# Loading the first input chunk of a split Fourier stage one unit earlier, ahead of the middle stage's loads

## The chip, the cores and the metric

The kernel runs on one core of a Trainium2 chip. Its engines are TensorE (PE in the profile; the weight loads of its matmuls have a row of their own, PEld), VectorE (DVE), ScalarE (ACT), GpSimd (POOL) and SyncE (SP), which here only issues DMAs. The metric is the device time of one execution in microseconds, the median of several runs. All data are float32.

## The reference

Two steps follow each other. The first is a global filter along the sequence: for each of 8 batches and 256 channels, a real Fourier transform over 3008 positions, a product with a complex filter, and the transform back. The second treats the 8 x 3008 = 24064 rows as tokens of a two-layer network with the activation h - tanh(h).

```python
X = np.fft.rfft(x, axis=1)                       # x: (8, 3008, 256)
y = np.fft.irfft(X * (filt_r + 1j * filt_i), n=3008, axis=1)
h = y.reshape(24064, 256) @ w_in                 # w_in: (256, 2048)
out = (h - np.tanh(h)) @ w_out                   # w_out: (2048, 256)
```

## The kernel before

The sequence length is factored as 64 x 47, and the transform is done by matmuls with small Fourier matrices, in stages that meet in DRAM. For batch `b`:

- The first stage turns `x` into the DRAM tensor `ct1[b]`. For batches 3 to 7 it is the generator `split_first` (line 306). It has three chunks `c`. Each chunk loads a piece of the matrix into a tile `f` (line 313) and two tiles `x0` and `x1`, both named `x_sb` in the profile (lines 320, 324, 326: eleven DMAs with the one for `f`, all on SP's queue); then DVE forms `x0 + x1` into a tile `a1` (line 331) and `x0 - x1` in place (line 333); 64 small matmuls follow into four PSUM banks with the tags `t`, `o1`, `y` and `o0` (line 340, tile `pm`); ACT and DVE combine the banks (lines 345 to 349), and eight stores to `ct1[b]` are put at the head of a list of stores. The tiles `f` and `x_sb` have two buffers each, so a new chunk's pair takes the place of the pair before.
- The middle stage, the generator `middle` (line 467), reads `ct1[b]` into a tile `a2` (line 374, four DMAs) and the filter into `ft` (line 382, 1 MB), works in four steps with matmuls at line 401, and writes `ct2[b]`.
- `last` (line 565) reads `ct2` by `load_e2` (lines 553 and 555) and makes the tokens' inputs with the matmuls of line 576.

The two-layer network is most of the work. Its tokens are cut into 48 groups (`groups`: batch `p` by chunk `c` of 0 to 5), and each group into four units `u` of 512 hidden columns. One loop over all 192 units `U` runs three things at once: `up` (first layer, matmuls at line 617, into banks `x`, `y`, `z`) for unit `U`, `shrink` (the activation, ACT lines 729 to 735, DVE line 739, and four GpSimd operations at lines 597 to 600) for unit `U - 1`, and `down` (second layer, matmuls at line 787, into banks `o0` to `o3`) for unit `U - 2`.

The instruction order on every engine is the order in which the program is written; nothing reorders it. Inside `up` there are five points `t(0)` to `t(4)`. Each issues up to four DMAs from the list of stores (line 894) on SP's queue and then takes one step of another generator. Which one is fixed by tables: if `(c, u, k)` is in the set `SPLIT_AT`, the next step of `split_first` for batch `p + 2` is taken, otherwise perhaps a step of `middle` for batch `p + 1`. A step of `split_first` is one of five per chunk: loads, sum, difference, matmuls with half of the combination, the other half. `SPLIT_AT` has 15 places for its 3 x 5 steps, and they hold for `p` = 1 to 5. Its first places are, in the order in which they are met:

```python
(0, 0, 2)  loads of chunk 0        (0, 1, 0)  sum, line 331
(0, 1, 1)  difference, line 333    (0, 1, 3)  matmuls, line 340
```

At the beginning of the last unit of the last group of a batch (`u == 3`, `c == 5`) the generators for the next batch are made. That of `middle` takes its first step there, which issues the loads of `a2` and `ft`; that of `split_first` is only made.

```python
if u == 3 and c + 1 == NC and p + 2 < BATCH:
    mids[p + 2] = middle(p + 2, zd4)
    next(mids[p + 2])
if u == 3 and c + 1 == NC and p + 3 < BATCH:
    firsts[p + 3] = split_first(p + 3, zd4)
```

SP's queue issues its DMAs strictly in order. Each of them waits on one of eight semaphores that are taken in turn, so a DMA is not issued before the one eight places ahead of it has landed.

Of the kernel before, what the change touches and what calls it, by code (L numbers as in the profile page):

```python
# [116 lines left out]
def kernel(  # L117
# [188 lines left out]
    def split_first(b, z):  # L306

        quarters = [slice(32 * k, 32 * k + 32) for k in range(4)]
        for c, tags in enumerate((("t", "o1", "y", "o0"), ("t", "o3", "o1", "o2"),
                                  ("t", "o1", "y", "o0"))):  # L310
            f = tr.tile([128, XH, 128], F32, tag="f", bufs=2, name="f")[:, 0:2]
            f = f.rearrange("p a (b n) -> p (a b) n", n=32)
            nc.sync.dma_start(f, split_d[:, 256 * c:256 * c + 256])
            x0, x1 = (tr.tile([128, XH, DM], F32, tag="x", bufs=2, name="x_sb") for _ in range(2))
            for h, t in enumerate((x0, x1)):
                at = b * SEQ + 32 * h * NR
                for g in range(2):
                    r = 2 * FH * c + FH * g
                    low, high = quarters[g], quarters[2 + g]
                    nc.sync.dma_start(t[low], dram(x.tensor, (at + r) * DM,  # L320
                                                   [[NR * DM, 32], [1, FH * DM]]))
                    lo = int(r == 0)
                    if lo:
                        nc.sync.dma_start(t[high, 0], dram(x.tensor, at * DM,
                                                           [[NR * DM, 32], [1, DM]]))
                    nc.sync.dma_start(t[high, lo:FH], dram(x.tensor, (at + NR - r - lo) * DM,
                                                           [[NR * DM, 32], [-DM, FH - lo], [1, DM]]))
            yield
            both = tr.tile([128, 2, 2, DM], F32, tag="a1", bufs=1, name="a1")
            even = both.rearrange("p v n c -> p (v n) c")  # L330
            V.tensor_add(even, x0, x1)
            yield
            V.tensor_sub(x1, x0, x1)
            yield
            banks = z(tags)
            for n in range(2):
                for k, (bank, part) in enumerate(zip(banks, quarters)):
                    for j, to in enumerate(quarters):
                        m, odd = 2 * (j // 2) + n, j % 2
                        nc.tensor.matmul(bank[to, n], f[part, 2 * m + odd],  # L340
                                         (x1 if odd else even)[part, m], start=True, stop=True)
            made = both, x0.rearrange("p (v n) c -> p v n c", v=2)
            other = x1[:, 0:2]
            for g, a1 in enumerate(made):
                ACT.copy(a1[:, 1], banks[2 + g])
            ACT.copy(other, banks[1])
            for g, a1 in enumerate(made):
                V.tensor_add(a1[:, 0], other if g else banks[0], a1[:, 1])
                V.tensor_sub(a1[:, 1], other if g else banks[0], a1[:, 1])
                outs[:0] = [(dram(ct1[b], ((1 - j % 2) * NH + 2 * FH * c + FH * g +  # L350
                                           2 * (j // 2)) * DM,
                                  [[2 * NH * DM, 32], [64 * NH * DM, 2], [1, 2 * DM]]),
                             a1[part].rearrange("p v n c -> p v (n c)"))
                            for j, part in enumerate(quarters)]
                yield

    SPLIT_AT = {(0, 0, 2), (0, 1, 0), (0, 1, 1), (0, 1, 3), (1, 1, 1), (1, 1, 4), (2, 0, 2),
                (3, 0, 2), (4, 2, 0), (4, 2, 2), (4, 3, 0), (5, 0, 2), (5, 1, 0), (5, 1, 3),
                (5, 2, 2)}

# [187 lines left out]
    def load_e2(b, c, parts=None, tiles=None):  # L548

        e2, gt = tiles or (tr.tile([128, CH, DM], F32, tag="e2", bufs=2, name="e2"),  # L550
                           tr.tile([128, CH, 64], F32, tag="gt", bufs=2, name="gt"))
        if tiles is None:
            nc.sync.dma_start(gt, (pairs_d if b else g_d)[:, CH * 64 * c:CH * 64 * (c + 1)])
        if parts is None:
            nc.sync.dma_start(e2, dram(ct2[b], CH * c * DM,
                                       [[(PAD if b else NH) * DM, 128], [1, CH * DM]]))
        return e2, gt
# [431 lines left out]
    with tc.tile_pool(name="tr", bufs=2) as tr, tc.manual_schedule():  # L989
# [260 lines left out]
        with tc.tile_pool(name="dn", bufs=2) as dn, \  # L1250
# [69 lines left out]
            for U in range(total + 2):  # L1320
                i, u = divmod(U, 4)
                if U == 6:
                    assert not pending
                    late = (None for u in (3, 5, 6, 7) for _ in sums(u))
                if U == 3:
                    G.dma_start(mats[:, 0:10 * PAD], wide_d[0:KM])
                if U < total:
                    p, c = groups[i]
                    if c == 0 and u == 0 and 0 < p < BATCH - 1:
                        plan += STAGES  # L1330
                    if u == 0 and i + 1 < len(groups) and c + 1 < NC:
                        e2s[i + 1] = load_e2(*groups[i + 1])
                    if u == 2 and i + 1 < len(groups) and c + 1 == NC:
                        assert not plan
                        e2s[i + 1] = load_e2(*groups[i + 1])
                    if u == 3 and c + 1 == NC and p + 2 < BATCH:
                        mids[p + 2] = middle(p + 2, zd4)
                        next(mids[p + 2])
                    if u == 3 and c + 1 == NC and p + 3 < BATCH:
                        firsts[p + 3] = split_first(p + 3, zd4)  # L1340
                sh = shrink(U - 1) if 0 <= U - 1 < total else iter(())
                dw = iter(())
                if 0 <= U - 2 < total:
                    dw = (down if U - 2 >= 4 else down_plain)(U - 2)

                def converting(n):

                    for _ in range(n):
                        if next(late, pending) is pending:
                            pending.clear()  # L1350

                def d():

                    next(dw, None)

                def e():

                    next(dw, None)
                    converting((U < 6) * (3 if U > 1 else 1))

                def s():

                    next(sh, None)

                def t(k):

                    store_some(4)
                    if k == 2 and stores:
                        store(*stores.pop())
                    if U >= total:  # L1370
                        return
                    pos = 20 * c + 5 * u + k
                    if i == 1 and pos == LEAD - 7:
                        assert not any(pending)
                        mids[1] = middle(1, zd4)
                        next(mids[1])
                        plan.extend(STAGES)
                    if (u, k) == (3, 2) and i + 1 < len(groups):
                        next(last(i + 1, z2))
                    elif due and due[0] <= pos and (U < 4 or u < 3 and k == 2):  # L1380
                        due.pop(0)
                        next(firsts[2])
                    elif (c, u, k) in SPLIT_AT and 0 < p < BATCH - 2:
                        next(firsts[p + 2])
                    elif plan and plan[0] == kinds.get((u, k)):
                        plan.pop(0)
                        next(mids[p + 1])
                    converting(2)
                    if k and U > 1:
                        next(copies, None)  # L1390
                        next(copies, None)

                if U < total:
                    if U == total - 1:
                        ones = cst.tile([128, 1], F32, name="ones")
                        G.memset(ones, 1.0)
                    (up if U >= 4 else up_plain)(U, d, e, s, t)
                else:
                    for k in range(5):
                        s()  # L1400
                        s()
                        d()
                        if U == total + 1 and k in (0, 2):
                            next(bound)
                        e()
                        t(k)
# [39 lines left out]
```

## Time and profile before

| | |
|---|---|
| median of 3 runs | 2573.39 us (2572.35 to 2575.72) |
| profiled execution | 2572.9 us, of which the span is 2571.1 us |
| TensorE matmul busy | 2542.1 us, 99% of the span |
| VectorE, ScalarE, GpSimd busy | 73%, 65%, 57% |
| granted TensorE clock, mean | 0.998 |
| DMA | 212.43 MB, 83 GB/s over the span |

All times in rows of the profile are microseconds from the start of the span unless they say ns. In a row of the timeline the columns are start, length, engine, line, operation, output and inputs, and the number of instructions merged into the row; in square brackets stands how long the engine was idle before and what ended that. A row of waits has who waited, for whom, the sum, the number of times and the longest one. A row of the windows view has the stretch, its length, the busy time of each engine with its number of instructions, the granted clock, and the DMA share and rate. Ends of matmuls are modelled, and a few records can be missing. One unit takes some 13 us, one batch of 24 units some 310 us.

### The profile page before, as it was taken

The numbers are of one execution on the slowest core, as the hardware profiler recorded it, in microseconds if no ns is written. First come the engines' busy times: TensorE is split into PE (matmuls) and PEld (weight loads), VectorE is DVE, ScalarE is ACT, GpSimd is POOL, SyncE is SP. The second block draws the span as 40 slices with busy tenths as digits, with TensorE's granted clock in tenths as the row PEclk, the third lists the DMA queues.
The fourth block names the chain that finished last, engine by engine and source line by source line (L and its number), as shares of the span: only waits on it lengthen the run. The fifth ranks groups of instructions, "written<-read, shape, count | busy, mean of one in ns | idle before, by whom it ended". The sixth has DMA issues, their size and how long they took to land.

```text
span 2571.1 us, 44601 instructions
## 1 busy us (share of the span) xinstructions
PE 2542.1 (99%) x17076; PEld 2171.9 (84%) x17076; DVE 1873.6 (73%) x2265; ACT 1667.3 (65%) x2497; POOL 1476.6 (57%) x1124
## 2 busy tenths in 40 slices
PE   8999999999999999999999999999999999999998
PEld 7678888888888888888888888888889888898887
DVE  6878777887678876788668886688866877555555
ACT  4566666666666666666666666666666666666665
POOL 4356665666456655566656665466645766555552
PEclk9999999999999999999999999999999999999999
DMA  8973214422343323342333322343123322110110
GB/s 222 270 186 102 64 41 102 119 66 54 77 113 91 81 53 86 89 105 69 72 88 88 99 67 60 94 111 95 37 60 90 93 66 50 28 32 18 26 21 19
DMA packets 333660, 212.43 MB, mean 83 GB/s; under 512 B 231738, under 2 KB 304856, under 8 KB 329790
## 3 DMA queue, kind: packets, MB, share of 16 engines
q1 hardware_dynamic: 318511, 184.59, 29.5%
q0 software_dynamic: 11424, 17.03, 2.5%
q10 hardware_dynamic: 3502, 7.87, 0.9%
q8 instruction: 136, 2.23, 0.4%
q14 instruction: 87, 0.70, 0.1%
HBM read 128.75 MB, written 83.39 MB: 83 GB/s over the span
## 4 chain that ended last, share of the span: by engine, by line
PE 87%; DMA 4%; DVE 3%; SPq 2%; POOL 1%; issue 1%; ACT 0%; DVEq 0%; POOLq 0%; ACTq 0%
PE o L787 40%; PE x L617 23%; PE z L617 11%; PE y L617 6%; PE pm L401 3%; PE pu L576 2%; SPq L894 1%; DMA ft<-filt 1%; PE pm L340 1%; DMA filt<-in_filt_r_dram 1%; DMA filt<-in_filt_i_dram 1%; DVE h L739 1%; DMA x<-in_x_dram 0%; DMA x_sb<-in_x_dram 0%; DMA a<-in_moe_w_out_dram 0%
## 5 line engine op out<-in xcount | busy, mean ns | idle before, releaser
L787 PE MATMUL o<-t,wd 128*128 128x256 f32 (+1 forms) x3008 | 763.2, 376 | 0.0
L597 POOL TENSOR_TENSOR t<-h 128x512 f32<-128x512 f32 (+1 forms) x186 | 305.8, 1644 | 707.1 <-DVE h L739 697.8
L739 DVE TENSOR_TENSOR h<-h,y 128x1024 f32<-128x1024 f32 (+1 forms) x384 | 579.1, 1508 | 159.4 <-ACT y L735 155.9
L787 PEld LDWEIGHTS o<-t,wd 128*128 128x128 f32 x3008 | 568.4, 190 | 86.3 <-POOL o L815 15.1
L617 PE MATMUL x<-tu,wu 128*128 128x256 f32 (+1 forms) x2256 | 576.2, 378 | 0.0
L787 PE MATMUL o<-h,wd 128*128 128x256 f32 (+1 forms) x2256 | 573.3, 377 | 1.8 <-DVE h L739 1.8
L787 PEld LDWEIGHTS o<-h,wd 128*128 128x128 f32 x2256 | 425.2, 190 | 73.6 <-issue 18.4
L623 ACT COPY s<-x 128x512 f32<-128x512 f32 (+1 forms) x188 | 108.8, 579 | 566.0 <-PE x L617 565.5
L617 PEld LDWEIGHTS x<-tu,wu 128*128 128x128 f32 x2256 | 423.0, 190 | 57.6 <-issue 3.9
L732 ACT ACTIVATE y<-y 128x1024 f32<-128x1024 f32 (+1 forms) x384 | 399.4, 1040 | 12.1
L735 ACT ACTIVATE y<-y 128x1024 f32<-128x1024 f32 (+1 forms) x384 | 399.8, 1041 | 4.6
L729 ACT ACTIVATE y<-h 128x1024 f32<-128x1024 f32 (+1 forms) x384 | 400.5, 1043 | 3.5 <-DVE h L665 1.7
L598 POOL TENSOR_TENSOR t<-h,t 128x512 f32<-128x512 f32 (+1 forms) x186 | 310.6, 1670 | 14.6
L600 POOL TENSOR_TENSOR t<-h,t 128x512 f32<-128x512 f32 (+1 forms) x186 | 301.5, 1621 | 0.0
L599 POOL TENSOR_TENSOR t<-h 128x512 f32<-128x512 f32 (+1 forms) x186 | 289.9, 1558 | 0.0
L623 ACT COPY u<-x 128x512 f32<-128x512 f32 (+1 forms) x376 | 213.7, 568 | 56.8 <-PE x L617 54.0
L665 DVE COPY h<-x 128x512 f32<-128x512 f32 (+1 forms) x188 | 127.8, 680 | 127.1 <-PE x L617 127.0
L617 PE MATMUL y<-ut,wu 128*128 128x256 f32 (+1 forms) x752 | 190.1, 375 | 0.8 <-ACT a L299 0.8
L617 PE MATMUL z<-ut,wu 128*128 128x256 f32 (+1 forms) x752 | 190.2, 375 | 0.5 <-DVE h L657 0.4
L617 PE MATMUL x<-ut,wu 128*128 128x256 f32 (+1 forms) x752 | 190.1, 375 | 0.6 <-DVE h L665 0.6
L617 PE MATMUL z<-tu,wu 128*128 128x256 f32 (+1 forms) x752 | 190.1, 375 | 0.4 <-DVE h L673 0.4
L657 DVE TENSOR_TENSOR h<-z,u 128x512 f32<-128x512 f32 (+1 forms) x188 | 127.2, 676 | 77.4 <-ACT u L623 77.1
(198 smaller groups left out, 2812.3 us busy)
## 6 DMA issues: line engine op xcount, KB each, us to landing
ft<-filt SPq DMA_DIRECT2D x28, 1024.0 KB
ct<-nn SPq DMA_DIRECT2D x56, 512.0 KB
e<-ct SPq DMA_DIRECT2D x47, 512.0 KB
a<-ct SPq DMA_DIRECT2D x112, 192.0 KB
out_dram<-ot SPq DMA_DIRECT2D x1248, 16.0 KB
x_sb<-in_x_dram SPq DMA_DIRECT2D x110, 128.0 KB
ct<-a SPq DMA_DIRECT2D x60, 128.0 KB
ct<-x_sb SPq DMA_DIRECT2D x60, 128.0 KB
```

Of the source, the lines that this page charges most:

```text
L597: by.tensor_sub(t[0], b[0][1], b[0][0])
L598: by.tensor_sub(t[1], b[1][1], t[0])
L599: by.tensor_sub(t[2], b[1][1], b[0][1])
L600: by.tensor_sub(t[3], b[1][0], t[1])
L617: nc.tensor.matmul(bank[:, k], wu[:, q - 1, (2 * u + k) * 128:(2 * u + k + 1) * 128], rhs[q - 1], start=(first and k == 0), stop=True, ski ...
L623: ACT.copy(t, X)
L665: V.tensor_copy(h[:, 2, :, 0:w], X)
L729: ACT.activation(y[k], ht[k], AF.Arctan, scale=TURN)
L732: ACT.activation(y[k], y[k], AF.Tanh, scale=BEND)
L735: ACT.activation(y[k], y[k], AF.Square, scale=SCALE, accum_out=y_sums[:, 2 * U + k // 2:2 * U + k // 2 + 1])
L739: V.tensor_mul(ht[k], ht[k], y[k])
L787: nc.tensor.matmul(product(q), wd[:, q - 1, (2 * u + k) * 128: (2 * u + k + 1) * 128], rhs[q - 1][:, k], start=(u == 0 and k == 0 and q == ...
```

## The change

The first step of `split_first` (the eleven loads of chunk 0) is taken where the generator is made, at the beginning of the last unit of the preceding batch's last group, and it is taken before the first step of `middle`, so that on SP's queue its eleven loads stand ahead of the loads of `a2` and `ft`. One place is taken out of `SPLIT_AT`, (0, 1, 1). The steps that remain for chunk 0 move forward by one place: the sum is taken at (0, 0, 2), the difference at (0, 1, 0); the matmuls stay at (0, 1, 3), and the other twelve steps stay where they were.

```diff
-    SPLIT_AT = {(0, 0, 2), (0, 1, 0), (0, 1, 1), (0, 1, 3), (1, 1, 1), (1, 1, 4), (2, 0, 2),
+    SPLIT_AT = {(0, 0, 2), (0, 1, 0), (0, 1, 3), (1, 1, 1), (1, 1, 4), (2, 0, 2),
                 (3, 0, 2), (4, 2, 0), (4, 2, 2), (4, 3, 0), (5, 0, 2), (5, 1, 0), (5, 1, 3),
                 (5, 2, 2)}
...
                         e2s[i + 1] = load_e2(*groups[i + 1])
+                    if u == 3 and c + 1 == NC and p + 3 < BATCH:
+                        firsts[p + 3] = split_first(p + 3, zd4)
+                        next(firsts[p + 3])
                     if u == 3 and c + 1 == NC and p + 2 < BATCH:
                         mids[p + 2] = middle(p + 2, zd4)
                         next(mids[p + 2])
-                    if u == 3 and c + 1 == NC and p + 3 < BATCH:
-                        firsts[p + 3] = split_first(p + 3, zd4)
```

No instruction is added or removed on any engine except for waits. On DVE, the order of the first two units of a batch becomes (line numbers of the kernel before): 739, **331**, 657, 665, 739, 673, **333**, 640, 802, 739, 808; it was 739, 657, 665, 739, 673, **331**, 640, 802, **333**, 739, 808.

## The prediction

> **What bounds the kernel now.** I read the page first: who is busy, and the chain that ended last.
>
> ```profile
> span 2571.1 us, 44601 instructions
> PE 2542.1 (99%) x17076; PEld 2171.9 (84%) x17076; DVE 1873.6 (73%) x2265; ACT 1667.3 (65%) x2497; POOL 1476.6 (57%) x1124
> PE 87%; DMA 4%; DVE 3%; SPq 2%; POOL 1%; issue 1%; ACT 0%; DVEq 0%; POOLq 0%; ACTq 0%
> ```
>
> TensorE is the bound nearly everywhere, so this change can win only the moments in which TensorE stands, or lose by making new ones. The view of waits says where the split first stage (lines 331 to 340) makes such moments.
>
> ```profile
> DVE a L331 <- DMA x_sb<-in_x_dram: 24.6, 4, 6.7
> PE pm L340 <- DVE o L808: 2.6, 4, 0.7
> PE pm L340 <- DVE x_sb L333: 0.8, 2, 0.5
> ```
>
> VectorE waits four times for `x` to land, 24.6 us in all, and behind this TensorE waits at the stage's matmuls. Four times, but the stage runs in five batches (`p` = 1 to 5): one batch shows it without the wait. To price the difference I took the stretch of each batch's first group, from the first matmul of one line 576 block to the first of the next, in the windows view. The rows are `p` = 1 to 5.
>
> ```profile
> 400.39:449.42 49.03, 49.03 (x386) 44.35 (x385) 36.61 (x45) 32.63 (x53) 25.89 (x21) 1.00 0.35 89
> 708.27:759.49 51.22, 50.17 (x385) 44.48 (x384) 33.91 (x46) 32.61 (x53) 24.04 (x21) 1.00 0.41 100
> 1018.35:1069.70 51.35, 50.17 (x385) 44.47 (x384) 33.91 (x46) 32.62 (x53) 24.01 (x21) 1.00 0.41 98
> 1328.56:1378.89 50.33, 49.62 (x386) 44.40 (x385) 33.93 (x46) 32.62 (x53) 24.02 (x21) 1.00 0.41 99
> 1637.74:1687.82 50.08, 49.57 (x385) 44.35 (x384) 33.93 (x46) 32.62 (x53) 24.01 (x21) 1.00 0.42 100
> ```
>
> The same work takes 49.03 us where VectorE does not wait and 51.22, 51.35, 50.33 and 50.08 where it does, at a granted clock of 1.00 in all of them. The whole excess lies at the line 340 block: from the last matmul group ahead of it to the first behind it is 2.28 us in `p` = 1 (427.07 to 429.35) and 4.50 in `p` = 2 (734.95 to 739.45).
>
> ```profile
> 427.07 0.92 PE L617 MATMUL x<-tu,wu 128*128 128x224 f32 x4
> ...
> 429.35 1.13 PE L787 MATMUL o<-t,wd 128*128 128x256 f32 x4
> ```
>
> ```profile
> 734.95 0.92 PE L617 MATMUL x<-tu,wu 128*128 128x224 f32 x4
> ...
> 739.45 1.13 PE L787 MATMUL o<-t,wd 128*128 128x256 f32 x4
> ```
>
> **The change part by part.** *The loads, 20 us earlier.* The timelines of SP and of VectorE in `p` = 2 show why `x` is late, with two rows of the chain for what lands when.
>
> ```profile
> 701.44 1.90 SPq L894 DMA_DIRECT2D out_dram<-ot  x4
> 703.82 1.73 SPq L374 DMA_DIRECT2D a<-ct  x4
> 705.60 0.38 SPq L382 DMA_DIRECT2D ft<-filt  x1
> ...
> 725.13 0.43 SPq L313 DMA_DIRECT2D f<-f_split  x1
> ...
> 730.88 0.42 SPq L326 DMA_DIRECT2D x_sb<-in_x_dram  x1
> ```
>
> ```profile
> 705.60 8.69 DMA ft<-filt
> ...
> 730.88 2.38 DMA x_sb<-in_x_dram
> ```
>
> ```profile
> 722.65 0.62 DVE L657 TENSOR_TENSOR h<-z,u 128x448 f32<-128x448 f32 x1 [1.25 <-ACT u L623]
> ...
> 726.24 0.62 DVE L673 TENSOR_TENSOR h<-z,u 128x448 f32<-128x448 f32 x1
> 733.48 1.23 DVE L331 TENSOR_TENSOR a<-x_sb 128x1024 f32<-128x1024 f32 x1 [6.62 <-DMA x_sb<-in_x_dram]
> ...
> 737.62 0.42 DVE L808 TENSOR_TENSOR o<-o,p 128x256 f32<-128x256 f32 x1
> ```
>
> The eleven loads are issued from 725.13, the last at 730.88, and it lands 2.38 us later, at 733.26; VectorE stood ready at 726.86 (726.24 + 0.62). It stands 6.62 us, and queued behind line 331 are 640, 802, 333, 739 and 808. Line 808 empties PSUM bank `o1`, which line 340 overwrites, so TensorE goes on only after 737.62 + 0.42 = 738.04. After the change the loads stand where 374 begins now, 703.82 (the copies into `ct1` that line 374 waits for are also the last readers of the tile, so nothing waits longer). Issuing them takes 730.88 + 0.42 - 725.13 = 6.2 us, to 710.0, and with the 2.38 the last lands at about 712.4. VectorE reaches line 331 at its new place when it falls idle before line 657, at 722.65 - 1.25 = 721.40: 9 us to spare. In `p` = 3 to 5 the program is the same, and the loads land with the same margin: the whole 24.6 us of waiting go.
>
> *What is late next: the PSUM banks.* `p` = 1 answers it: line 331 without a wait, line 808 done before the block.
>
> ```profile
> 419.03 1.91 DVE L331 TENSOR_TENSOR a<-x_sb 128x1024 f32<-128x1024 f32 x1
> ...
> 426.40 0.41 DVE L808 TENSOR_TENSOR o<-o,p 128x256 f32<-128x256 f32 x1
> ```
>
> Line 808 ends at 426.40 + 0.41 = 426.81, before TensorE so much as begins the group ahead of the block, at 427.07. So no wait of that kind is left, and 49.03 us is the level: gain (51.22 + 51.35 + 50.33 + 50.08) - 4 x 49.03 = **6.86 us**. `p` = 1 gains nothing, since it has no wait to lose.
>
> Does a later wait take it back? The stretch is bounded by blocks of TensorE, whose work outside it is unchanged, and `p` = 1 and 2 go on from it with no stall carried over: the excess is in the stretch and no shorter one follows. I count the whole.
>
> A second, smaller price comes from TensorE's idle rows alone: 2.6 + 0.8 = 3.4 us. They count the time after the modelled end of a matmul; the stretches go by starts, so I take 6.86 and keep 3.4 as the lower end. The Trainium skill, "Perfetto Trace Analysis", section "Tensor Engine Instruction (MATMUL, LD_WEIGHTS)", says that the start of a matmul is recorded but its end is computed from its size. By that rule idle rows undercount; the trace agrees, 2.2 us more from start to start in `p` = 2 where the busy column leaves 51.22 - 50.17 = 1.05.
>
> *Line 331, ahead of 657.* At 721.40 VectorE is idle until 722.65, and 1.23 us fits there to 0.02. The profile's group view gives the length of line 331 over all chunks, and GpSimd's timeline what runs beside it.
>
> ```profile
> L331 DVE TENSOR_TENSOR a<-x_sb x15: 1211/1226/2301, 419.0 to 1908.9; 128x1024 f32<-128x1024 f32 x15
> ```
>
> ```profile
> 726.47 1.27 POOL L597 TENSOR_TENSOR t<-h 128x512 f32<-128x512 f32 x1 [6.16 <-DVE h L739]
> ```
>
> It can take 2.30 us. Then 657 ends at 721.40 + 2.30 + 0.62 = 724.32, and the matmuls that overwrite its bank `z` follow at 725.23:
>
> ```profile
> 725.23 0.92 PE L617 MATMUL z<-ut,wu 128*128 128x224 f32 x4
> ```
>
> That leaves 0.9 us: cost 0. GpSimd is idle from 720.31 to 726.47, so I expect 1.23.
>
> *Line 333, ahead of 640 and 802.* It now starts at 726.24 + 0.62 = 726.86, beside GpSimd's run from 726.47, so up to about 2.3 us, to 729.2; 640 follows to 729.8. The next writer of its bank `y` is line 340, behind the group of 734.95: cost 0. Lines 802 and 808 no longer have 333 between them, so 808 comes sooner than in `p` = 1, if at all different.
>
> Were both moved operations at their longest and their slacks gone, the excess over 1.21 us would fall on TensorE: 2 x (2.30 - 1.21) x 5 batches = 10.9 us. With slacks of 0.9 us and 5 us none of it does. The Trainium skill, "SBUF — State Buffer", section "Who interferes with whom", speaks against the two moves: a VectorE operation with two SBUF inputs and a GpSimd operation that reads SBUF hold each other off for a whole instruction. The trace agrees that line 331 has two lengths.
>
> *What waits behind the eleven loads on SP.* `a2`, `ft`, 20 output stores, and `gt` and `e2` of the next group are issued 6.2 us later, and a little more, since at most eight DMAs are on the way at once. The `ft` load lands at 714.29 now and would at about 720.5. Their users:
>
> ```profile
> 742.78 1.37 PE L401 MATMUL pm<-a,mats_sb 24*32 24x512 f32 x32
> ```
>
> Line 401 needs `a2` at 742.78 (740.6 after the gain), `ft` later still: 20 us of cover. `e2`, issued ahead of 725.13 now, is read by the line 576 block at 759.49 that ends the stretch of `p` = 2: 34 us ahead now, some 26 then. If that cover were gone each microsecond would be one of TensorE in each of five batches. By the time of the stores that follow, SP has made up the 6.2 us, because the eleven loads are missing there. In `p` = 0 the first loads move into batch 0's last unit; same order, same cover. Cost 0. The few waits added to instructions (line 340 and a transpose now name DMAs which landed long before) I bound by line 331, which starts at 733.48, 0.22 us after its last load landed at 733.26, with all its waits: at two such instructions in five batches 0 to 2.2 us. I take 0: a wait on something long done is nearer to a check than to that row, which ends a real wait.
>
> **Sum.** 2572.9 - 6.86 = 2566.0 for the profiled execution, which stands 0.5 us under the median of 2573.39; against the median, 2566.5 us, or 0.27% faster.
>
> **The rivals.** A difference under 0.2%, 5.1 us, is about what a measurement of this kernel cannot tell from none.
>
> *Half the gain.* TensorE gains only its idle rows, 3.4 us, because another wait takes the place of 808's at the block: 2570.0 us. For it: the block waits for several VectorE results. Against: `p` = 1, the same program, 49.03 us.
>
> *Late at the new place (slower).* The loads might not have landed at 721.40, because they wait for the copies out of the old tile and share the DMA engines with `a2` and `ft`. Then line 657 stands behind 331, and `z` is freed late. It decides when `x` lands after 725.23 - 0.62 - 1.23 = 723.4, that is 11 us later than I reckon. With as long a wait as now, 6.62, 331 would start at 728.0, `z` be free at 729.9, and TensorE lose 4.7 us in each of five batches: 23.5 - 6.9 = 16.6 slower, 2590 us. Against: the whole set lands within 8.1 us of its first issue in `p` = 2.
>
> *The pair exclusion*, as priced above: 2566.5 + 10.9 = 2577. It needs both slacks gone.
>
> *It changes nothing.* If the matmul block was limited by other evictions, all four excesses would remain: 2573. `p` = 1 speaks against it.
>
> **How the numbers follow.** Full gain 0.69, half 0.15, nothing 0.05, late 0.06, exclusion 0.05. The full case has its own range, 2564.5 to 2568.5: the sum with up to 2 us for the added waits downwards of the gain, 1.5 us for the spread of medians, and some tenths more from an earlier 808. With 0.15 and 0.05 of the others taken in, the range is 2564.0 to 2573.0, a little over 0.8 of the cases. Faster by over 0.2% needs 5.1 of the 6.9 us; a few of the full cases fall under it: 0.65. Within 0.2%: 0.24. Slower: 0.11.
>
> **What would show it.** Right: no row of line 331 waiting for `x`; line 340 without the waits for 808 and 333; the four stretches at 49.0 us; the eleven loads on SP's timeline ahead of line 374 and `ft` landing some 6 us later with no reader waiting. Wrong: a wait of 331 at its new place, a wait of TensorE's `z` or `y` matmuls for 657 or 640, or one of line 401 for `a2`; or stretches above 50 us with the waits gone, which would put the excess elsewhere than VectorE's lateness.

## The result, and the profile after

The changed kernel takes 2564.38 us (median of 7 runs, 2563.03 to 2568.16) against 2573.39 us (7 runs, 2571.99 to 2577.16): a ratio of 0.9967, 95% interval 0.9955 to 0.9978. It is faster by 9.0 us, where 6.9 were forecast. From the page of its profiled execution, the span, the busy time of each engine, and the chain that ended last by engine:

```profile
span 2564.4 us, 44624 instructions
...
PE 2540.9 (99%) x17076; PEld 2177.8 (85%) x17076; DVE 1878.4 (73%) x2265; ACT 1666.3 (65%) x2497; POOL 1481.4 (58%) x1124
...
PE 94%; DMA 2%; DVE 1%; ACT 1%; issue 1%; POOL 0%; ACTq 0%; POOLq 0%; DVEq 0%
```

The share of TensorE in the chain that ended last goes from 87% to 94%; the shares of DMA (4% to 2%), of VectorE (3% to 1%) and of SP's queue (2% to none in this line) are the main ones that shrink. The five stretches, in the windows view of the changed kernel:

```profile
400.99:450.01 49.02, 49.02 (x386) 44.38 (x385) 35.30 (x45) 32.61 (x53) 25.72 (x21) 1.00 0.38 86
708.86:757.88 49.02, 49.02 (x385) 44.37 (x384) 35.33 (x46) 32.61 (x53) 25.73 (x21) 1.00 0.43 102
1016.74:1065.76 49.02, 49.02 (x386) 44.38 (x385) 35.33 (x46) 32.60 (x53) 25.73 (x21) 1.00 0.45 103
1324.61:1373.63 49.02, 49.02 (x386) 44.38 (x385) 35.31 (x46) 32.62 (x53) 25.71 (x21) 1.00 0.44 100
1632.48:1681.50 49.02, 49.02 (x385) 44.38 (x384) 35.31 (x46) 32.61 (x53) 25.71 (x21) 1.00 0.45 101
```

All five are 49.02 us, with TensorE busy throughout. Batch 2 of the changed kernel (its first group begins 0.59 us later in the span, at 708.86 instead of 708.27), on SP's queue:

```profile
703.96 0.44 SPq L313 DMA_DIRECT2D f<-f_split  x1
...
708.96 0.42 SPq L326 DMA_DIRECT2D x_sb<-in_x_dram  x1
709.42 1.71 SPq L374 DMA_DIRECT2D a<-ct  x4
711.18 0.38 SPq L382 DMA_DIRECT2D ft<-filt  x1
711.60 14.22 SPq L894 DMA_DIRECT2D out_dram<-ot  x20
```

The timeline of VectorE in the same place, and of TensorE where it overwrites the banks that VectorE frees:

```profile
719.98 1.99 DVE L739 TENSOR_TENSOR h<-h,y 128x1024 f32<-128x1024 f32 x1 [2.31 <-ACT y L735]
721.90 1.21 DVE L331 TENSOR_TENSOR a<-x_sb 128x1024 f32<-128x1024 f32 x1
723.23 0.63 DVE L657 TENSOR_TENSOR h<-z,u 128x448 f32<-128x448 f32 x1
...
727.36 2.04 DVE L333 TENSOR_TENSOR x_sb<-x_sb 128x1024 f32<-128x1024 f32 x1
729.33 0.61 DVE L640 TENSOR_TENSOR h<-y,s 128x448 f32<-128x448 f32 x1
...
733.93 0.42 DVE L808 TENSOR_TENSOR o<-o,p 128x256 f32<-128x256 f32 x1 [1.21 <-ACT p L807]
```

```profile
725.82 0.92 PE L617 MATMUL z<-ut,wu 128*128 128x224 f32 x4
726.57 0.92 PE L617 MATMUL x<-ut,wu 128*128 128x224 f32 x4
...
735.54 0.92 PE L617 MATMUL x<-tu,wu 128*128 128x224 f32 x4
...
737.81 1.13 PE L787 MATMUL o<-t,wd 128*128 128x256 f32 x4
738.78 0.92 PE L617 MATMUL z<-ut,wu 128*128 128x224 f32 x4
...
741.14 1.47 PE L401 MATMUL pm<-a,mats_sb 24*32 24x512 f32 x32
```

Line 331 fills the gap that VectorE had ahead of line 657 and does not wait: by the trace's semaphore updates the last `x` load lands at 713.34, 8.6 us before line 331 starts at 721.90. That is the smallest margin of the five batches; the others have 10.3 to 13.5 us. Line 808 is done at 734.35, before the group of 735.54, and TensorE passes the block in 2.27 us (735.54 to 737.81), without a row that waits for VectorE.

### The profile page after: what moved, and what is told of

Read it like the earlier page. It is cut to its first block, busy times and chain, and to the rows that moved or that the text cites. A ratio compares the mean times of both kernels' runs of the same rounds, so it can differ in the third digit from the quotient of the medians.

```text
span 2564.4 us, 44624 instructions
## 1 busy us (share of the span) xinstructions
PE 2540.9 (99%) x17076; PEld 2177.8 (85%) x17076; DVE 1878.4 (73%) x2265; ACT 1666.3 (65%) x2497; POOL 1481.4 (58%) x1124
## 4 chain that ended last, share of the span: by engine, by line
PE 94%; DMA 2%; DVE 1%; ACT 1%; issue 1%; POOL 0%; ACTq 0%; POOLq 0%; DVEq 0%
PE o L787 43%; PE x L617 25%; PE z L617 12%; PE y L617 6%; PE pm L401 3%; PE pu L576 2%; DMA ct<-a 1%; PE pm L340 1%; DMA raw<-in_moe_w_in_dram 0%; DMA fh<-f 0%; DMA mats_sb<-mats 0%; PE pe L1089 0%; PE o L842 0%; PE pf L297 0%; PE warm L1038 0%
## 5 line engine op out<-in xcount | busy, mean ns | idle before, releaser
L597 POOL TENSOR_TENSOR t<-h 128x512 f32<-128x512 f32 (+1 forms) x186 | 305.7, 1643 | 712.4 <-DVE h L739 703.9
```

Of the source, the lines that this page charges most:

```text
L597: by.tensor_sub(t[0], b[0][1], b[0][0])
```

## The experiments

Two questions: is VectorE's lateness at the block the whole cause, and why is the measured gain 9.0 us when the stretches give 6.9? Stretches of the experiments are from the start of one line 576 block to the next, as in the prediction.

**Behind the middle stage's loads.** The two first steps swapped:

```diff
-  if u == 3 and c + 1 == NC and p + 3 < BATCH:
-      firsts[p + 3] = split_first(p + 3, zd4)
-      next(firsts[p + 3])
   if u == 3 and c + 1 == NC and p + 2 < BATCH:
       mids[p + 2] = middle(p + 2, zd4)
       next(mids[p + 2])
+  if u == 3 and c + 1 == NC and p + 3 < BATCH:
+      firsts[p + 3] = split_first(p + 3, zd4)
+      next(firsts[p + 3])
```

> The changed kernel with the two generators' first steps swapped: the eleven loads of chunk 0 are issued at the same unit, but behind the loads of a2 and ft instead of ahead of them. Theory (only the landing before line 331's place counts): the loads are issued some 2.2 us later and share the engines with ft, land some 4 to 8 us later than in the changed kernel, at about 716 to 720 in batch 2, still ahead of 721.9 where VectorE reaches line 331; all five first-group stretches stay at 49.0 us and the time is that of the changed kernel, 2564 to 2567 us, ratio to the kernel before about 0.9970. Rival (the place ahead of the middle stage's loads is needed): line 331 waits again, line 657 behind it frees bank z late, the stretches go over 49.5 us.

2564.78 us (7 runs), 0.9957 (0.9941 to 0.9972) of the kernel before, whose 21 runs in this series have a median of 2575.41 us. All five stretches are 49.02 us. SP and VectorE in its batch 2:

```profile
704.57 0.38 SPq L382 DMA_DIRECT2D ft<-filt  x1
...
715.46 0.42 SPq L326 DMA_DIRECT2D x_sb<-in_x_dram  x1
```

```profile
720.26 1.21 DVE L331 TENSOR_TENSOR a<-x_sb 128x1024 f32<-128x1024 f32 x1
```

Behind `ft` the last `x` load is issued 8.1 us later than in the changed kernel by the start of the group (715.46 - 707.23 = 8.23 us behind it, against 708.96 - 708.86 = 0.10). It lands at 717.87, 2.4 us before line 331. In batches 1 to 5 this margin is 5.1, 2.4, 1.8, 1.3 and 0.4 us, where the changed kernel has 13.5, 8.6, 10.3, 10.9 and 10.9. So the place ahead of the middle stage's loads is worth no time in these runs, since nothing waits in either order, but it is worth most of the margin: in batch 5 of this variant the loads are just in time.

**The loads alone.** Sum and difference stay where the kernel before has them:

```diff
-    SPLIT_AT = {(0, 0, 2), (0, 1, 0), (0, 1, 3), (1, 1, 1), ...
+    SPLIT_AT = {(0, 1, 0), (0, 1, 1), (0, 1, 3), (1, 1, 1), ...
```

> Only the loads are moved: issued where the changed kernel has them, while the sum and the difference are taken at the places of the kernel before, (0, 1, 0) and (0, 1, 1). Theory (VectorE's wait for x was the whole cause): stretches of 49.0 us in all five batches, as batch 1 of the kernel before had them with these places, ratio about 0.9970, and the time within 1 us or so of the changed kernel. Rival (the earlier sum and difference carry part of the gain, by taking 333 out from between 802 and 808): line 340 waits for 808 or 813 again, stretches of 49.1 to 50 us, 1 to 4 us of the gain missing.

2565.96 us (9 runs), 0.9960 (0.9947 to 0.9973). Five stretches of 49.02 us. In its batch 2:

```profile
727.99 2.04 DVE L331 TENSOR_TENSOR a<-x_sb 128x1024 f32<-128x1024 f32 x1
...
731.44 2.05 DVE L333 TENSOR_TENSOR x_sb<-x_sb 128x1024 f32<-128x1024 f32 x1
...
735.49 0.41 DVE L808 TENSOR_TENSOR o<-o,p 128x256 f32<-128x256 f32 x1
```

Line 808 comes 0.9 us later than in the changed kernel by the start of the group (735.49 - 709.48 = 26.0 against 733.93 - 708.86 = 25.1), and that is still early enough. So the move of sum and difference carries none of the gain that these runs can show: the wait for `x` was the cause.

**Four sums, and two.** The sum of chunk 0 repeated at its place, with no value changed:

```diff
-            V.tensor_add(even, x0, x1)
+            for _ in range(4 if c == 0 else 1):
+                V.tensor_add(even, x0, x1)
```

> The changed kernel with the sum of chunk 0 (line 331) computed four times over at its place, which lengthens it by 3 x 1.21 = 3.6 us and changes no value. It measures the slack that the prediction put behind this place. Theory: line 331 starts at 721.9 in batch 2, four of them end at 726.7, line 657 ends at 727.4, and the z matmuls due at 725.8 start 1.6 us late: stretches of 50.6 us in all five batches, 5 x 1.6 = 8 us on top of the changed kernel, about 2572 us. Rival A (VectorE's idle time covers it all): 49.0 us and 2564 us. Rival B (there is no slack): 3.6 us per batch, 18 us, 2582 us.

> The changed kernel with the sum of chunk 0 computed twice, 1.2 us longer, no value changed. The slack behind the place of line 331 by the trace of the changed kernel: line 657 ends at 723.86 in batch 2 and the z matmuls are due at 725.84, 1.98 us. Theory (the slack is real): stretches of 49.0 us in all five batches. Rival (every VectorE microsecond at this place counts): 50.2 us, 6 us in all.

With four sums the time is 2573.81 us (10 runs), 0.9991 (0.9980 to 1.0002), and the stretches are 50.79, 50.80, 50.78, 50.79 and 50.79 us, 1.77 above 49.02. The extra line shifts the numbers below it by one, so 658 and 618 here are 657 and 617 elsewhere:

```profile
726.02 4.99 DVE L332 TENSOR_TENSOR a<-x_sb 128x1024 f32<-128x1024 f32 x4
730.93 0.62 DVE L658 TENSOR_TENSOR h<-z,u 128x448 f32<-128x448 f32 x1
```

```profile
731.61 1.02 PE L618 MATMUL z<-ut,wu 128*128 128x224 f32 x4 [1.51 <-DVE h L658]
```

With two sums (2566.35 us, one run) the stretches are 49.02, 49.02, 49.02, 49.03 and 49.02. Three more sums add 4.99 - 1.21 = 3.78 us to VectorE and 1.77 to TensorE: the slack is 2.0 us, as the trace has it (line 657 ends at 723.86, `z` is due at 725.82), and what goes beyond it falls on TensorE (3.78 - 1.77 = 2.0), in the bank that the prediction named.

**Late at the new place, on purpose.** Loads at the beginning of the batch itself, sum at its new place:

```diff
-    SPLIT_AT = {(0, 0, 2), (0, 1, 0), (0, 1, 1), (0, 1, 3), ...      # kernel before
+    SPLIT_AT = {(0, 0, 0), (0, 0, 2), (0, 1, 0), (0, 1, 3), ...
```

> The rival of the prediction that the loads land late at the new place of the sum, made on purpose: loads at (0, 0, 0) of the batch itself, sum at (0, 0, 2), difference at (0, 1, 0). The loads are issued only some 2 us earlier than in the kernel before and should land at about 731.4 in batch 2, while VectorE stands at line 331 from 721.9. Theory (line 657 is queued behind 331 and frees bank z): the z matmuls of line 617, due at 725.8, start after 731.4 + 1.2 + 0.6 = 733.3, so 7.5 us more in each of batches 2 to 5 and 1 to 2 us in batch 1: stretches of 56 to 58 us, 2564 + 4 x 7.5 + 1.5 = 2596 us, slower than both kernels. Rival (TensorE has other cover there, only the line 340 block matters): stretches under 51 us and a time under 2573 us.

2610.41 us (4 runs), 1.0135 (1.0111 to 1.0159): slower, by the mechanism expected, and by more. The stretches are 54.53, 58.78, 59.53, 58.87 and 57.89 us, in batches 2 to 5 8.9 to 10.5 above 49.02 where 7.5 were expected, and 5.5 in batch 1 where 1 to 2 were. TensorE in batch 2, and three windows of it:

```profile
736.36 1.86 PE L617 MATMUL z<-ut,wu 128*128 128x224 f32 x4 [6.89 <-DVE h L657]
738.01 1.70 PE L617 MATMUL x<-ut,wu 128*128 128x224 f32 x4
```

```profile
728.00:730.00 2.00, 1.47 (x8) 1.01 (x6) 0.00 (x0) 0.00 (x0) 0.00 (x0) 1.00 0.75 197
...
738.00:740.00 2.00, 2.00 (x7) 1.78 (x6) 1.75 (x2) 0.25 (x1) 1.81 (x2) 0.50 0.04 8
...
742.00:744.00 2.00, 2.00 (x11) 1.87 (x10) 0.27 (x1) 0.79 (x3) 2.00 (x2) 1.00 0.00 0
```

The wait for line 657 is there, 6.89 us of idle time. At its end and behind it the granted clock is 0.50, and the group of `z` takes 1.65 us from its start to the next one's (736.36 to 738.01), where in the changed kernel it takes 0.75 us (725.82 to 726.57). This second part of the cost was in no sum of mine. The two parts add up: from the start of the group the `z` matmuls begin 7.05 us later than in the changed kernel (736.36 - 712.35 = 24.01 against 725.82 - 708.86 = 16.96), close to the 7.5 expected; and the clock is at half from 734.86 to 741.69, 5.3 us of it behind the start of `z`, which at half speed loses 2.7. Together that is 9.7 of the 9.8 us.

**The loads of the middle stage late.** In the changed kernel, the first step of `middle` is taken at (0, 1, 4) of the batch that uses it:

```diff
   if u == 3 and c + 1 == NC and p + 2 < BATCH:
       mids[p + 2] = middle(p + 2, zd4)
-      next(mids[p + 2])
...
+  if (c, u, k) == (0, 1, 4) and 0 < p < BATCH - 1:
+      next(mids[p + 1])
```

> The changed kernel with the first step of the middle stage, the loads of a2 and ft, taken at (0, 1, 4) of the batch that uses them instead of a unit before it: behind the stores of the line 340 block on SP's queue, some 30 us later than in the changed kernel. It shows what the cover of these loads is and what it costs when it is gone. Theory: issued at about 742 in batch 2, a2 lands at about 745, where line 401 is due at 740.6: TensorE waits some 4 to 5 us in each of six batches, 24 to 30 us in all, about 2590 us; ft lands some 9 us after its issue and holds only VectorE. Rival (nothing in the middle stage is due so soon): stretches of 49 us, 2564 us.

2625.0 us (one run). The stretches are 60.62, 61.33, 59.97, 60.99 and 59.75 us, 57.6 us over five times 49.02, where 24 to 30 us were expected over six batches. Batch 6, which has no split stage, keeps its 47.2 us: no stores of that stage stand ahead of the loads, and they are issued 10.3 us after the start of its first group, against 32.9 us in batch 2 (754.64 - 721.70). In batch 2:

```profile
754.64 1.75 SPq L374 DMA_DIRECT2D a<-ct  x4
```

```profile
758.17 6.63 PE L401 MATMUL pm<-a,mats_sb 24*32 24x512 f32 x32 [4.12 <-DMA a<-ct]
764.73 3.35 PE L787 MATMUL o<-h,wd 128*128 128x224 f32 x8
```

```profile
757.00:761.00 4.00, 2.83 (x16) 0.45 (x16) 0.00 (x0) 0.00 (x0) 2.17 (x3) 0.51 1.14 187
```

The idle row of 4.12 us is what was expected as the whole wait, but the cost is 12.3 us in this batch (61.33 - 49.02). The row ends with the first of the four loads of `a2`, which lands at 758.04; by the trace's semaphore updates the others land at 759.16, 761.21 and 762.83, and line 401 stops for the third and the fourth again. Its block is over at 764.73, 9.4 us later than in the changed kernel by the start of the group (764.73 - 721.70 = 43.03 against 742.54 - 708.86 = 33.68). The clock is at half from 757.12 to 770.77, and the groups behind the block, up to 770.83, lose another 3.0 us. So the cover of these loads is real; the price without it is the landing of the last load and the clock, not the idle row. How much of the 9.4 us inside the block is late loads and how much is the clock is not separated here.

**More executions of the kernel before, and one of the changed one.** No edit.

> The kernel before, unchanged, profiled in a second execution. The median gain of the changed kernel, 9.0 us, is above the 6.9 us that the stretches of the first profile give. Theory A (the landing of x varies from execution to execution, and the first profile caught an early one): the sum of the five stretches over 49.02 us differs from 6.9 us by 1 us or more in this execution or the next. Theory B (the excess is the same in each execution, and what varies lies elsewhere, ahead of the batches that are compared): the sum stays at 6.9 us within 0.5 us, and the start of the first stretch moves by 1 us or more.

> A third execution of the kernel before, for the same two theories: A, the sum of the stretches over 49.02 us differs from 6.9 us by 1 us or more in at least one of the two; B, 6.9 us within 0.5 us in both.

> A fourth execution of the kernel before. Its runs spread from 2570.6 to 2584.3 us, those of the changed kernel from 2563.0 to 2568.2, and three profiles of it, 2570.0 to 2571.1 us of span, are from the lower half. Theory A: in its longer executions x lands later, TensorE stands longer at the line 340 block, and the granted clock falls there as it did behind the idle of 7 us in the experiment with the late loads; an execution over 2576 us shows first-group stretches whose sum over 5 x 49.02 us is above 9 us, with a granted clock below 1.00 in at least one. Theory B: the stretches keep their sum of 6.9 to 7.5 us at any length, and the difference lies ahead of the first stretch.

> A fifth execution of the kernel before, for the same two theories: A, an execution over 2576 us has its excess in the first-group stretches, with a lower granted clock; B, it has it ahead of 400 us of the span.

> A sixth execution of the kernel before, for the same two theories, A and B as for the fifth.

> A second execution of the changed kernel. By theory A and B alike its five stretches are 49.02 us again, since nothing waits for x; its span differs from the first profile's 2564.4 us only by where the first stretch begins, 400.99 us there.

The table gives, for each profiled execution, the start of the first stretch, the five stretches, and their sum over 5 x 49.02 us.

| | time, us | first starts | stretches, us | sum over |
|---|---|---|---|---|
| before, first profile | 2572.9 | 400.39 | 49.03, 51.22, 51.35, 50.33, 50.08 | 6.9 |
| before, second | 2572.64 | 399.78 | 49.02, 51.40, 51.61, 50.71, 49.88 | 7.5 |
| before, third | 2571.75 | 398.36 | 49.02, 50.96, 51.51, 50.60, 50.41 | 7.4 |
| before, fourth | 2579.2 | 400.23 | 49.02, 54.38, 55.20, 50.34, 49.76 | 13.6 |
| before, fifth | 2576.78 | 398.61 | 49.02, 52.42, 54.87, 50.45, 50.10 | 11.8 |
| before, sixth | 2576.67 | 402.81 | 49.03, 50.25, 52.10, 51.37, 50.46 | 8.1 |
| changed, second | 2567.19 | 401.85 | 49.02, 49.02, 49.03, 49.03, 49.02 | 0.0 |

The second and third execution fit neither theory well (0.5 to 0.6 us more than the first). The fourth and fifth are as theory A expected, 13.6 and 11.8 us with a lower granted clock. The sixth is between: 1.2 us of its excess over the first profile lie in the stretches, 2.4 us ahead of them, where its clock is at half for 6.83 us twice and that of the first profile for 3.41 us once. The windows of the fourth execution, VectorE in its batches 2 and 3, and TensorE and the clock in batch 3:

```profile
708.10:762.48 54.38, 53.02 (x386) 46.21 (x385) 34.02 (x46) 32.62 (x53) 23.99 (x21) 0.94 0.40 94
1021.33:1076.53 55.20, 53.07 (x385) 46.19 (x385) 34.02 (x46) 32.62 (x53) 23.98 (x21) 0.94 0.39 91
1335.38:1385.72 50.34, 49.63 (x386) 44.40 (x385) 33.92 (x46) 32.63 (x53) 24.04 (x21) 1.00 0.42 99
```

```profile
733.61 1.23 DVE L331 TENSOR_TENSOR a<-x_sb 128x1024 f32<-128x1024 f32 x1 [6.92 <-DMA x_sb<-in_x_dram]
...
1047.69 1.22 DVE L331 TENSOR_TENSOR a<-x_sb 128x1024 f32<-128x1024 f32 x1 [7.76 <-DMA x_sb<-in_x_dram]
```

```profile
1050.97 0.40 PE L340 MATMUL pm<-x_sb,f 32*32 32x256 f32 x1 [1.39 <-DVE x_sb L333]
...
1052.30 0.63 PE L340 MATMUL pm<-a,f 32*32 32x256 f32 x1 [0.71 <-DVE o L808]
...
1054.55 2.08 PE L787 MATMUL o<-t,wd 128*128 128x256 f32 x4
```

```profile
1050.00:1052.00 2.00, 0.63 (x6) 0.14 (x6) 2.00 (x3) 0.00 (x0) 0.00 (x0) 1.00 0.00 0
1052.00:1054.00 2.00, 1.70 (x56) 0.97 (x56) 1.97 (x5) 0.00 (x0) 0.73 (x1) 0.50 0.00 0
```

VectorE waits 7.76 us in batch 3, 1.0 more than in the same batch of the first profile (6.74), and TensorE stands 1.39 and 0.71 us with a handful of small matmuls between. Then the clock falls to 0.50, and the stretch is 3.85 us longer than in the first profile, for one microsecond of lateness. In batch 2 VectorE waits 6.92 us, 0.3 more than in the first profile, and the stretch is 3.2 us longer.

The six executions let the two parts be told apart. In the twenty stretches of batches 2 to 5 in which the clock stays at 1.00, the excess over 49.02 us is VectorE's wait less 4.4 us, to within 0.02 us (a wait of 6.62 us gives 2.20, one of 7.50 us 3.09): VectorE can be 4.4 us late there at no cost, and beyond that each microsecond counts once. By this rule the lateness is worth 6.9, 7.5, 7.4, 7.9, 8.0 and 8.1 us in the six executions. The remaining 5.7 us of the fourth and 3.7 us of the fifth lie in the four stretches in which the clock is at half for 3.41 or 6.83 us. So the landing of `x` does vary, but what varies most is whether the clock falls behind the wait.

The six sums have a mean of 9.2 us, near the measured 9.0. This is no sharp test: the sums spread from 6.9 to 13.6 us, the start of the first stretch varies by 4.5 us, and the median of the kernel before moved from 2573.39 to 2575.41 us between the two series.

## Why the prediction was right

- **The cause** (VectorE's wait for `x` ahead of the line 340 block): shown. Without it all stretches are 49.02 us, whether the loads stand ahead of or behind those of the middle stage, and whether sum and difference move or not; with it, and with the clock at 1.00, the excess follows the length of the wait.
- **The level of 49.03 us** from batch 1: measured 49.02 or 49.03 in five of five batches, in both profiles of the changed kernel.
- **Landing and margin.** Reckoned: issue from 703.82 to 710.0, landing at about 712.4, 9 us to spare. Measured: issue from 703.96 to 709.38, landing at 713.34, 8.6 us to spare. The `ft` load is issued 5.0 us later by the start of the group (2.32 us behind it, where it was 2.67 ahead of it), forecast 6.2, and nobody waits for it. The prediction did not ask what the order of the two sets on the queue is worth: no time here, but behind the middle stage's loads the margin goes down to 0.4 us.
- **Line 331 ahead of 657** was priced at 0 with 0.9 us left if it took 2.30, which makes 2.0 us for the expected 1.23. It took 1.21, and the slack is 2.0 us by the experiment.
- **The pair exclusion**: the lengthening that the prediction priced shows at line 333 and cost nothing, as forecast. Line 333 took 2.04 us beside GpSimd, where line 331 took 1.21 alone, and the GpSimd operation beside it took 2.14 us instead of 1.27.

```profile
728.40 2.14 POOL L598 TENSOR_TENSOR t<-h,t 128x512 f32<-128x512 f32 x1
```

- **The sum of 6.86 us** is the term that was mis-sized. It is what one execution showed, the least late of six (6.9 to 8.1 us by lateness alone), and it has no term for the granted clock, which fell behind the wait in two of the six and added 5.7 and 3.7 us. With both, the six executions give 6.9 to 13.6 us, on the mean 9.2, against 9.0 measured between the medians. The result lies 2.1 us under the 2566.5 us of the sum and only 0.4 us inside the range. That the range reached so far is in part luck: its lower end was made of the spread of medians and of an earlier line 808, not of these two, and the experiment with the loads alone shows no gain from the earlier line 808. The 2 us kept for the added waits were not needed: all stretches are at 49.02 us, and the rest of the span is no longer than before.
- **The price from TensorE's idle rows**, 3.4 us, kept as the lower end and as a rival, was not a bound of anything: it is less than any execution showed. The stretches, by starts, were the right reading.
- **Late at the new place** and **the cover of the middle stage's loads** were priced microsecond for microsecond. The prediction reckoned 4.7 us per batch for the first, the expectation of the experiment 7.5; batches 2 to 5 show 8.9 to 10.5. The experiments bear out the places (bank `z`, `a2`) and not the price. For `z` the missing part is the clock: 2.7 us in batch 2, on a lateness of 7.05. For `a2`, 12.3 us beside an idle row of 4.1, it is the clock and the later three of the four loads.

## What to carry to other kernels

Where one batch of a repeated program runs without the wait, the difference between equal stretches prices the change better than the sum of idle rows. A wait for a transfer should be priced from more than one execution: its length varies a little, and whether the clock falls behind it varies more. An idle row that ends with one of several loads is not the whole wait. And when two orders of the loads give the same time, their margins should be compared before one is called free: here 8.6 us or more were left in one order and 0.4 us in the other.

## What the runs showed of the hardware

A wait of TensorE can cost more than itself, because the granted clock falls to 0.50 during it or just behind it. In the experiment with the late loads it was at half for 3.41 us with 3.55 us of idle time, and for 6.83 us with 6.5 to 8.5 us. In the experiment with the late loads of the middle stage it was at half for 10.2 or 13.7 us with idle rows of 4.0 to 4.4 us, with late loads holding up the matmuls behind them. In the kernel before it was at half for 6.83 us after 0.65 and 0.71 us of idle time, and after 1.39 and 0.71 us, with a few small matmuls in between. After 1.5 us in the experiment with four sums, and after 1.2 and 0.7 us in the sixth execution of the kernel before (its stretch of 52.10 us has a mean clock of 1.00), it stayed at 1.00. The Trainium skill, "TensorE: Matmul & The Clock Gate", section "HAM oscillation — how this bites in real kernels", warns of idle gaps over some 3.4 us; these rows agree for the long ones, and show that two short gaps close together can do it too. Why two such gaps do it in one execution and not in another is not settled here. The idle times alone do not decide it: 0.65 and 0.71 us were enough in the fourth execution, and 0.72 and 0.71 us in the second (its stretch of 51.61 us) were not.
